# Block forms copied by VectorE, results by tokens, and a check that comes later

## The chip, the cores and the metric

One core of one Trainium2 chip runs the whole program. The metric is device microseconds of one execution, the median of several. TensorE (PE) multiplies into PSUM, VectorE (DVE), ScalarE (ACT) and GpSimd (POOL) do the elementwise work, and SyncE (SP) issues all transfers on one queue.

## The reference

Four batches, 8 heads, 768 tokens, head size 48. A gated linear attention feeds a soft mixture of 8 experts and a dense layer:

```python
f = 1.0 / (1.0 + np.exp(-f_logit))
for t in range(S):
    state = f[:, :, t, :, None] * state + np.einsum('bhd,bhe->bhde', k[:, :, t], v[:, :, t])
    y[:, :, t] = np.einsum('bhd,bhde->bhe', q[:, :, t], state)
...
logits = x @ phi                       # x: y as 3072 tokens x 384
slot_in = softmax(logits, 0).T @ x     # 32 slots, 4 of each expert
slot_out[e] = np.maximum(slot_in[e] @ w1[e], 0.0) @ w2[e]
x = softmax(logits, 1) @ slot_out
...
h = x @ w_in
return (h - np.tanh(h)) @ w_out
```

## The kernel before

**Attention** works in 16 groups g: two pairs of heads, 384 tokens each, cut into three chunks of 128 tokens. A chunk of a group is a step i, 48 in all; g and c are i divided by 3. In q, k and the decays the head size lies on partitions: head 0 of a pair on partitions 0 to 47, head 1 on 64 to 111, and 2 pairs x 3 chunks x 128 tokens in the 768 columns. Six steps share a run of tokens; the first of a run has no old state, the last makes no new one.

`prep` loads f, k, q, makes the running decays (exp, ln on ScalarE, a scan on VectorE, L287, two exps) and multiplies k and q by them, mostly on GpSimd (L260, a helper's line: ks and qs). So that one matmul gives the scores of both heads of a pair, q must also stand in a block form bd: each head's part in columns of its own, zeros in the other's. For groups 0 and 1 VectorE writes it; from group 2 on two transfers within SBUF copy q into it, 48 partitions x 6 pieces of 512 bytes each:

```python
r48 = slice(h * 64, h * 64 + 48)
dma(ring("bd", g)[r48].rearrange("p (x h j) -> p h x j", x=6, h=2)[:, h], Q6[r48])
```

`step` does the rest, by names that the plan uses: P, scores of 128 keys x 128 queries for 2 pairs x 2 heads (L361); ev, their masking out of PSUM by VectorE (L375); K, the transpose of the decayed keys (L370), and kh, ScalarE's copy of it (L379); U, the new state's part, one head at a time in 64 of the 128 stationary columns (L387); sadd and ss, the state's sum and decay on VectorE (L398, L396; L403); Q, the old state times q (L410); Y, values times masked scores, with the values as stationary operand (48 columns, L418), so that results come out with the head size on partitions; yt, ScalarE's copy of them (L423); T, two transposes to tokens on partitions (L428); x, the copy into the activations (L433).

The order of all this is not written by hand: `Plan` takes each operation's engine, cost, dependencies and due time, schedules them in a list, and fixes each engine's order, SyncE's transfers and the prefetches of weights among them. An engine then works strictly in that order. Costs and due times are numbers in the `add` calls.

After attention come token transposes (L1583) and logits, the softmax and slots, the experts (L1866 on) whose weights arrive meanwhile, and the gates. The **dense stage** (`dense`) is a loop of 96 iterations, 6 parts of 512 tokens by 16 blocks: one hidden matmul (L1987), a square on ScalarE (L1993), a product on VectorE (L1994), three output matmuls (L2003). `hook(i, ...)` hangs other work behind iteration i: the conversion of the last weights (va, vb, vc), sums over them (w_mm, w_end), the closing of the first two parts (f_zero), and a check of how large gates and slots are (k_gates to k_ok), which decides whether the fast path's result stands. Of that check `k_gates(0)` is a product on GpSimd, `k_gates(1)` its sum on VectorE, `k_nc` two tiny matmuls with VectorE between them.

Of the kernel before, what the change touches and what calls it, by code (L numbers as in the profile page):

```python
# [173 lines left out]
def arena_map():  # L174
# [8 lines left out]
    for n, w in [("e1_0", 774), ("e1_1", 774), ("rs_0", 774), ("rs_1", 774),  # L183
# [4 lines left out]
                 ("kh_0", 1728), ("kt_0", 256), ("kt_1", 256), ("kt_2", 256), ("yt_0", 256), ("yt_1", 256), ("yt_2", 256),  # L188
# [6 lines left out]
def attention(nc, A, AR, x_all, ident, pcs, BK, plans):  # L195
    amap, _ = arena_map()
    W = {"e1": 774, "rs": 774, "k": 768, "q": 768, "vr": 576, "bd": 1536, "s": 192, "sx": 256, "kt": 256, "yt": 256,
         "pm": 512}
    NB = {"e1": 2, "rs": 2, "k": NKQ, "q": NQ, "vr": 2, "bd": 2, "s": 1, "sx": 3, "kt": 3, "yt": 3, "pm": 3}
# [22 lines left out]
    def vv(i, r, h):  # L222
        gi, c = divmod(i, 3)
        return ring("vr", gi).rearrange("p (c r h e) -> p c r h e", c=3, r=2, h=2)[:, c, r, h]
# [4 lines left out]
    def dma(out, in_):  # L229
        nc.sync.dma_start(out=out, in_=in_)  # L230
# [16 lines left out]
    for i in range(4, 7):  # L247
        add(("zb", i), "dve", 0.36, lambda i=i: memset("dve", BK[i][:, 0:256], 0.0))
# [16 lines left out]
    def prep(g):  # L265
# [63 lines left out]
        for i, x in enumerate(halves):  # L329
            e = EQS.get((g, i), "pool")  # L330
            add(("qs", g, i), e, tt(e, 384), lambda x=x, e=e: mul(e, Q6[:, x], Q6[:, x], X6[:, x]),
                ("q", g), ("e2", g, 0), ("bd", g, 0), ("bd", g, 1))
        if g > 1:
            def bdma():
                for h in range(2):
                    r48 = slice(h * 64, h * 64 + 48)
                    dma(ring("bd", g)[r48].rearrange("p (x h j) -> p h x j", x=6, h=2)[:, h], Q6[r48])

            add(("bd", g), "dma", 0.82, bdma, ("qs", g, 0), ("qs", g, 1), ("P", 3 * g - 4), ("P", 3 * g - 5), ("P", 3 * g - 6))
# [5 lines left out]
    def step(i):  # L345
# [34 lines left out]
        four = lambda a: a.rearrange("p (r h e) -> p r h e", r=2, h=2)[:, :, :, 0:48]  # L380
        ub = BK[4][:, 0:256]
        u = four(ub)
        if not last:
            def mmU():
                for pr in range(2):
                    for h in range(2):
                        nc.tensor.matmul(u[h * 64:h * 64 + 64, pr, h], lhsT=ktk[:, pr, h * 64:h * 64 + 64],  # L387
                                         rhs=vv(i, pr, h), start=pr == 0, stop=pr == 1)

            sn = ring("s", i).rearrange("p (r h e) -> p r h e", r=2, h=2)  # L390
            sp = four(ring("sx", i))
            sp1 = four(ring("sx", i + 1))
            g1, c1 = divmod(i + 1, 3)
            add(("U", i), "pe", 0.4, mmU, ("kh", i), ("v", g), ("sadd", i - 1), ("sadd", i - 2), ("zb", 4))
# [1903 lines left out]
```

## Time and profile before

| | |
|---|---|
| timed runs | 381.83, 384.38, 388.3 us; median 384.38 us |
| the profiled execution's own time | 380.08 us |
| its span, first to last instruction | 378.4 us |
| busy: TensorE, VectorE, ScalarE, GpSimd | 315.3, 240.1, 206.9, 113.3 us |
| mean granted clock of TensorE | 0.951 |
| bytes moved | 67.1 MB, mean 177 GB/s |

All rows are of that one profiled execution, in us from the span's start. Busy shares are means over stages that have different limits, so they are read by stage. A wait is put down to what came last before it ended. In the chain of work that ended last, each piece is what released the next one.

### The profile page before, as it was taken

Reading aid. Unit: us, or ns where it says so; the run is one execution under the profiler, and the core shown is the slowest. Engines: PE = TensorE matmul, PEld = TensorE weight load, DVE = VectorE, ACT = ScalarE, POOL = GpSimd, SP = SyncE. Lnnn points to the kernel's source line nnn. Section 1 sums busy time; section 2 is a strip of 40 time slices with the busy share of each in tenths; the row PEclk is TensorE's granted clock in tenths of the full one; section 3 lists DMA queues with packets and bytes.
Section 4 is the critical chain, followed back from the end, with each engine's and each line's share of the span. In section 5 each row is a group of like instructions: output and inputs, shape, how many; then the busy total and the mean of one; then the engine's idle time right before and its main releaser. Section 6 shows DMA issues by size and latency. Waiting matters only on the chain.

```text
span 378.4 us, 6422 instructions
## 1 busy us (share of the span) xinstructions
PE 315.3 (83%) x2350; PEld 223.6 (59%) x2350; DVE 240.1 (63%) x400; ACT 206.9 (55%) x402; POOL 113.3 (30%) x136
## 2 busy tenths in 40 slices
PE   2988888566469999999989989787957999999991
PEld 1666666455347777777844444654645566778780
DVE  5976676645153744443587993799835469877770
ACT  5655877446351543333477844996541434666651
POOL 7465897342314452000000000345991002000000
PEclk9998999999786999999999999989995999999996
DMA  7978999999999655776418999400000004211202
GB/s 268 323 177 206 270 261 272 272 241 253 260 274 287 172 144 145 224 252 245 193 38 337 425 423 422 193 1 0 0 2 0 0 2 168 83 47 39 83 0 92
DMA packets 26392, 67.10 MB, mean 177 GB/s; under 512 B 3216, under 2 KB 11664, under 8 KB 24688
## 3 DMA queue, kind: packets, MB, share of 16 engines
q1 hardware_dynamic: 26352, 66.61, 57.5%
q8 instruction: 20, 0.33, 0.4%
q14 instruction: 20, 0.16, 0.1%
HBM read 57.75 MB, written 4.72 MB: 165 GB/s over the span
## 4 chain that ended last, share of the span: by engine, by line
PE 40%; DMA 22%; DVE 13%; ACT 8%; POOL 7%; issue 5%; SPq 2%; POOLq 0%; DVEq 0%; ACTq 0%
PE bank L2003 11%; DMA slab_AR<-v 6%; PE bank L361 6%; DMA slab_AR<-wo 5%; DMA slab_AR<-k 4%; DVE r_WA L1994 4%; PE bank L1987 4%; PE bank L418 3%; PE bank L1866 3%; DMA slab_WA<-wi 3%; PE bank L410 3%; POOL slab_AR L1734 3%; POOL slab_AR L260 2%; DMA slab_XA<-f 2%; SPq L230 2%
## 5 line engine op out<-in xcount | busy, mean ns | idle before, releaser
L260 POOL TENSOR_TENSOR slab_AR<-slab_AR 128x384 f32<-128x384 f32 (+1 forms) x65 | 67.1, 1058 | 67.5 <-DMA slab_AR<-k 39.8
L1994 DVE SCALAR_TENSOR_TENSOR r_WA<-bank,slab_AR,slab_WA 128x512 fp32r<-128x512 f32 x96 | 70.4, 749 | 23.8 <-ACT slab_WA L1993 23.3
L1993 ACT ACTIVATE slab_WA<-bank 128x512 f32<-128x512 f32 x96 | 56.9, 598 | 49.2 <-PE bank L1987 49.2
L2003 PE MATMUL bank<-r_WA,r_AR 128*128 128x512 f32 x216 | 66.7, 414 | 12.6 <-DVE r_WA L1994 10.0
L361 PE MATMUL bank<-slab_AR 128*128 128x256 f32 x192 | 54.9, 412 | 3.1 <-DMA slab_AR<-slab_AR 1.6
L2003 PEld LDWEIGHTS bank<-r_WA,r_AR 128*128 128x128 f32 x216 | 40.2, 193 | 28.7 <-DVE r_WA L1994 9.7
L375 DVE TENSOR_TENSOR slab_AR<-bank,slab_AR 128x512 f32<-128x512 f32 x48 | 32.8, 684 | 36.8 <-PE bank L361 36.7
L361 PEld LDWEIGHTS bank<-slab_AR 128*128 128x128 f32 x192 | 34.7, 201 | 10.8 <-issue 3.4
L287 DVE TENSOR_TENSOR_SCAN slab_AR<-slab_XA,slab_AR 128x774 f32<-128x774 f32 (+1 forms) x18 | 31.5, 1750 | 13.0 <-ACT slab_XA L284 10.9
L1987 PE MATMUL bank<-r_AR,r_XA 128*128 128x512 f32 x96 | 38.6, 407 | 0.1
L418 PE MATMUL bank<-slab_AR 128*48 128x128 f32 x384 | 32.1, 290 | 2.5 <-DMA slab_AR<-v 2.5
L428 PE MATMUL bank<-ident,slab_AR 128*128 128x128 f32 x96 | 20.1, 294 | 13.4 <-ACT slab_AR L423 13.1
L433 ACT COPY slab_XA<-bank 128x192 f32<-128x192 f32 x48 | 15.2, 318 | 28.4 <-PE bank L428 28.2
L410 PE MATMUL bank<-slab_AR 128*128 128x128 f32 x160 | 27.1, 294 | 2.1 <-DVE slab_AR L403 2.1
L423 ACT COPY slab_AR<-bank 128x256 f32<-128x256 f32 x48 | 17.9, 372 | 15.2 <-PE bank L418 14.4
L410 PEld LDWEIGHTS bank<-slab_AR 128*128 128x128 f32 x160 | 23.4, 201 | 4.7 <-DVE slab_AR L403 3.0
L418 PEld LDWEIGHTS bank<-slab_AR 128*48 128x48 f32 x384 | 20.0, 128 | 9.9 <-issue 5.2
L387 PE MATMUL bank<-slab_AR 128*64 128x48 f32 x320 | 18.1, 236 | 7.5 <-DMA slab_AR<-v 5.2
L2003 PE MATMUL bank<-r_WA,r_XA 128*128 128x512 f32 x72 | 23.4, 425 | 0.9 <-DVE r_WA L1994 0.9
L290 ACT ACTIVATE slab_AR<-slab_AR 128x774 f32<-128x774 f32 (+1 forms) x18 | 14.0, 778 | 17.8 <-POOL slab_AR L260 10.4
L370 PE MATMUL bank<-ident,slab_AR 128*128 128x128 f32 x80 | 17.9, 308 | 6.7 <-POOL slab_AR L260 6.7
L282 ACT ACTIVATE slab_XA<-slab_XA 128x768 f32<-128x768 f32 (+1 forms) x18 | 14.0, 776 | 17.4 <-DMA slab_XA<-f 7.4
(223 smaller groups left out, 486.1 us busy)
## 6 DMA issues: line engine op xcount, KB each, us to landing
slab_AR<-w SPq DMA_DIRECT2D x5, 1536.0 KB, 7.6
slab_WA<-w SPq DMA_DIRECT2D x12, 512.0 KB, 7.1
slab_AR<-v SPq DMA_DIRECT2D x16, 288.0 KB, 5.7
slab_WA<-wi SPq DMA_DIRECT2D x9, 512.0 KB, 7.7
slab_AR<-wo SPq DMA_DIRECT2D x3, 1536.0 KB, 20.4
out<-slab_WA SPq DMA_DIRECT2D x17, 256.0 KB, 2.1
slab_XA<-f SPq DMA_DIRECT2D x28, 144.0 KB, 6.9
slab_AR<-slab_AR SPq DMA_DIRECT2D x28, 144.0 KB, 5.6
```

The source lines that it names most:

```text
L260: (nc.vector if eng == "dve" else nc.gpsimd).tensor_tensor(out=out, in0=i0, in1=i1, op=ALU.mult)
L287: lambda fs=fs: nc.vector.tensor_tensor_scan(out=ring("rs", g)[:, fs], data0=gt[:, fs], data1=cap[:, fs], initial=0.0, op0=ALU.add, op1=AL ...
L361: nc.tensor.matmul(P.rearrange("p (r h j) -> p r h j", r=2, h=2)[:, pr], lhsT=kv(g)[:, pr, c], rhs=bds[g % 2][R, :, pr, c], start=True, st ...
L375: lambda: nc.vector.tensor_tensor(out=pm, in0=P.rearrange("p (g j) -> p g j", g=4), op=ALU.mult, in1=mask.rearrange("p (g j) -> p g j", g= ...
L387: nc.tensor.matmul(u[h * 64:h * 64 + 64, pr, h], lhsT=ktk[:, pr, h * 64:h * 64 + 64], rhs=vv(i, pr, h), start=pr == 0, stop=pr == 1)
L410: nc.tensor.matmul(y[:, pr], lhsT=ring("sx", i).rearrange("p (r e) -> p r e", r=2)[:, pr], rhs=qv(g)[:, pr, c], start=pr == 0, stop=False)
L418: nc.tensor.matmul(y[h * 64:h * 64 + 48, pr], lhsT=vv(i, pr, h), rhs=pm[:, pr * 2 + h], start=first and pr == 0, stop=pr == 1)
L428: nc.tensor.transpose(out=tb[:, pr * 128:pr * 128 + 128], in_=yt[:, pr * 128:pr * 128 + 128], identity=ident)
L1987: nc.tensor.matmul(h, lhsT=M4[:, fb * 128:fb * 128 + 128], rhs=cT[tg], start=True, stop=True)
L1993: nc.scalar.activation(v, h, AF.Square, scale=THIRD)
L1994: nc.vector.scalar_tensor_tensor(out=r, in0=h, scalar=uu[:, fb:fb + 1], in1=v, op0=ALU.add, op1=ALU.mult)
L2003: nc.tensor.matmul(facc[o], lhsT=w, rhs=r, start=fb == 0, stop=fb == 15 and tg < 2)
```

## The change

1. From group 2 on the block form is written by two copies of 64 partitions x 768 columns on VectorE instead of two transfers; each waits, as the transfers did, for qs and for the score matmuls of the steps that used the buffer before.
2. In Y the masked scores are the stationary operand (128 columns) and the values, 48 columns, the moving one. Results come out with tokens on partitions. Q gets q as the stationary and the state as the moving operand (96 columns). yt and T fall away, with three memsets, the buffer yt and the use of one PSUM bank; x copies straight out of the bank of Y, and Q and Y now wait for x of two steps before.
3. U takes both heads of a pair in one matmul: 128 stationary columns, 96 moving ones. Half of what it makes isn't used. sadd and ss become two operations each, one for each half of the partitions.
4. The check's pieces are hung behind later iterations, k_gates from 18 and 22 to 34 and 39, the others after.
5. The first of the token transposes no longer waits for the last steps, since its bank is free.

```diff
         if g > 1:
-            def bdma():
-                for h in range(2):
-                    r48 = slice(h * 64, h * 64 + 48)
-                    dma(ring("bd", g)[r48].rearrange("p (x h j) -> p h x j", x=6, h=2)[:, h], Q6[r48])
-
-            add(("bd", g), "dma", 0.82, bdma, ("qs", g, 0), ("qs", g, 1), ("P", 3 * g - 4), ("P", 3 * g - 5), ("P", 3 * g - 6))
+            for h in range(2):
+                rr = slice(h * 64, h * 64 + 64)
+                add(("bd", g, h), "dve", 0.5,
+                    lambda h=h, rr=rr: nc.vector.tensor_copy(
+                        ring("bd", g)[rr].rearrange("p (x h j) -> p h x j", x=6, h=2)[:, h], Q6[rr]),
+                    ("qs", g, 0), ("qs", g, 1), ("P", 3 * g - 4), ("P", 3 * g - 5), ("P", 3 * g - 6))
...
                 for pr in range(2):
-                    for h in range(2):
-                        nc.tensor.matmul(u[h * 64:h * 64 + 64, pr, h], lhsT=ktk[:, pr, h * 64:h * 64 + 64],
-                                         rhs=vv(i, pr, h), start=pr == 0, stop=pr == 1)
+                    nc.tensor.matmul(u[:, pr].rearrange("p h e -> p (h e)"), lhsT=ktk[:, pr], rhs=vv(i, pr), start=pr == 0,
+                                     stop=pr == 1)
...
-            add(("U", i), "pe", 0.4, mmU, ("kh", i), ("v", g), ("sadd", i - 1), ("sadd", i - 2), ("zb", 4))
...
+            add(("U", i), "pe", 0.5, mmU, ("kh", i), ("v", g), ("sadd", i - 1, 0), ("sadd", i - 1, 1))
+
+            def add_s(h):
+                rr = slice(h * 64, h * 64 + 64)
+                if first:
+                    nc.vector.tensor_copy(sn[rr], u[rr, :, h])
+                else:
+                    nc.vector.tensor_tensor(out=sn[rr], in0=sp0[rr, :, h], in1=u[rr, :, h], op=ALU.add)
...
+            for h in range(2):
+                add(("sadd", i, h), "dve", 0.2, lambda h=h: add_s(h), ("U", i), ("ss", i - 1, h))
+            for h in range(2):
+                add(("ss", i, h), "dve", 0.25, lambda h=h: scale_s(h), ("sadd", i, h), ("pcs", g1),
+                    ("Q", i - 2), ("zs", (i + 1) % 3))
...
-                    nc.tensor.matmul(y[:, pr], lhsT=ring("sx", i).rearrange("p (r e) -> p r e", r=2)[:, pr],
-                                     rhs=qv(g)[:, pr, c], start=pr == 0, stop=False)
-
-            add(("Q", i), "pe", 0.45, mmQ, ("ss", i - 1), *qsk, ("yt", i - 2))
+                    nc.tensor.matmul(y[:, pr].rearrange("p h e -> p (h e)"), lhsT=qv(g)[:, pr, c],
+                                     rhs=ring("sx", i)[:, 0:192].rearrange("p (r e) -> p r e", r=2)[:, pr], start=pr == 0,
+                                     stop=False)
+
+            add(("Q", i), "pe", 0.5, mmQ, ("ss", i - 1, 0), ("ss", i - 1, 1), *qsk, ("x", i - 2))
...
-                    nc.tensor.matmul(y[h * 64:h * 64 + 48, pr], lhsT=vv(i, pr, h), rhs=pm[:, pr * 2 + h],
-                                     start=first and pr == 0, stop=pr == 1)
-
-        add(("Y", i), "pe", 0.6, mmY, ("ev", i), ("v", g), ("Q", i), ("yt", i - 2), ("Y", i - 1), ("zb", 5), ("zb", 6))
-        yt = ring("yt", i)
-        add(("yt", i), "act", 0.33, lambda: nc.scalar.copy(yt, BK[5 + i % 2][:, 0:256]), ("Y", i), ("T", i - 3))
...
-        add(("T", i), "pe", 0.44, mmT, ("yt", i), ("x", i - 2), "ident")
+                    w = pr * 2 + h
+                    nc.tensor.matmul(y[:, pr, h], lhsT=pm[:, w], rhs=vv(i, pr)[:, h * 48:h * 48 + 48],
+                                     start=first and w == 0, stop=w == 3)
+
+        add(("Y", i), "pe", 0.9, mmY, ("ev", i), ("v", g), ("Q", i), ("x", i - 2), ("Y", i - 1))
...
-        add(("x", i), "act", 0.3, lambda: nc.scalar.copy(dst, four(tb)), ("T", i),
+        add(("x", i), "act", 0.3, lambda: nc.scalar.copy(dst, y.rearrange("p r h e -> p (r h e)")), ("Y", i),
...
-        bank_free = [[("x", 46), ("x", 47)], [("ev", 46)], [("ev", 47)], [("kh", 46)]]
+        bank_free = [[], [("ev", 46)], [("ev", 47)], [("kh", 46)]]
...
-        hook(18, k_gates, 0)
-        hook(22, k_gates, 1)
+        hook(34, k_gates, 0)
+        hook(39, k_gates, 1)
...
-        hook(27, k_nc)
-        hook(34, k_slots, 0)
-        hook(38, k_slots, 1)
-        hook(40, k_bound, 0)
-        hook(45, k_bound, 1)
-        hook(50, k_flags)
-        hook(54, k_ok)
+        hook(44, k_nc)
+        hook(44, k_slots, 0)
+        hook(49, k_slots, 1)
+        hook(51, k_bound, 0)
+        hook(58, k_bound, 1)
+        hook(61, k_flags)
+        hook(64, k_ok)
```

## Rows read from the trace of the kernel before

**Rows 1.** Stretches of the whole run: busy us of each engine, clock, DMA share, GB/s.

```profile
0.00:40.00 40.00, 28.32 (x213) 20.98 (x214) 28.73 (x46) 25.16 (x54) 24.53 (x40) 0.96 0.86 245
40.00:120.00 80.00, 57.65 (x504) 43.88 (x505) 41.01 (x62) 43.47 (x91) 38.96 (x42) 0.91 1.06 263
120.00:178.60 58.60, 57.38 (x526) 44.23 (x525) 29.58 (x56) 23.21 (x64) 14.66 (x16) 1.00 0.65 200
...
202.60:241.50 38.90, 36.35 (x331) 17.58 (x332) 30.27 (x56) 24.22 (x38) 2.59 (x3) 1.00 0.96 392
...
279.60:294.00 14.40, 7.98 (x20) 5.63 (x21) 6.04 (x11) 2.39 (x4) 4.41 (x4) 0.64 0.00 0
```

**Rows 2.** Chain that ended last, 30 to 48 us: start, length, what.

```profile
34.98 4.73 DMA slab_AR<-slab_AR
```

**Rows 3.** DMA issues from 0 to 120 us: count, KB each, median us to landing.

```profile
slab_AR<-slab_AR SPq DMA_DIRECT2D x18, 144.0 KB, 7.5
```

**Rows 4.** Timeline of the dense stage, 276 to 290 us, VectorE and TensorE.

```profile
276.62 0.86 PE L2003 MATMUL bank<-r_WA,r_AR 128*128 128x512 f32 x3
...
277.55 0.86 PE L2003 MATMUL bank<-r_WA,r_AR 128*128 128x512 f32 x3
...
283.00 0.95 DVE L2037 TENSOR_REDUCE slab_AR<-slab_WA 128x24 f32<-128x768 f32 x1 [5.73 <-POOL slab_WA L2035]
...
284.88 1.65 PE L2003 MATMUL bank<-r_WA,r_AR 128*128 128x512 f32 x3 [5.30 <-DVE r_WA L1994]
...
286.88 0.58 PE L2042 MATMUL bank<-ident,chk 128*1 128x128 f32 x2
...
288.61 0.58 PE L2044 MATMUL bank<-chk,slab_AR 1*128 1x1 f32 x2 [1.14 <-DVE chk L2043]
```

**Rows 5.** One stretch of 2 us in which a block form is transferred.

```profile
159.00:161.00 2.00, 2.00 (x20) 1.59 (x20) 0.43 (x2) 1.03 (x4) 0.00 (x0) 1.00 1.08 221
```

**Rows 6.** Waits of the whole run: us in total, times, longest.

```profile
POOL slab_AR L260 <- DMA slab_AR<-k: 39.8, 7, 9.4
...
PE bank L428 <- ACT slab_AR L423: 13.1, 8, 5.5
```

**Rows 7.** Chain that ended last, 135 to 158 us: TensorE's pieces of a step.

```profile
135.66 1.06 PE bank L361 x4
...
140.15 0.22 PE bank L370 x2
...
147.50 0.45 PE bank L410 x4
147.95 0.37 PE bank L387 x8
148.32 0.37 PE bank L428 x2
148.68 0.57 PE bank L418 x8
...
157.01 0.87 PE bank L361 x4
```

**Rows 8.** Timeline of weight loads of the slot sums.

```profile
199.81 1.64 PEld L1702 LDWEIGHTS bank<-slab_AR 128*128 128x128 f32 x14 [0.21 <-DVE slab_AR L1694]
```

**Rows 9.** Three lines: duration in ns, min/median/max, first and last start, shapes.

```profile
L317 DVE COPY slab_AR<-slab_AR x4: 259/289/291, 9.6 to 13.9; 64x256 f32<-64x256 f32 x4
...
L403 DVE TENSOR_TENSOR slab_AR<-slab_AR,pcs x40: 347/358/1082, 14.3 to 171.8; 128x192 f32<-128x192 f32 x40
...
L260 POOL TENSOR_TENSOR slab_AR<-slab_AR x65: 682/952/2462, 6.0 to 147.6; 128x384 f32<-128x384 f32 x60, 128x256 f32<-128x256 f32 x5
```

**Rows 10.** Timeline of VectorE, 202 to 203 us: a 96-wide operation.

```profile
202.26 0.26 DVE L1820 TENSOR_TENSOR slab_AR<-bank,slab_AR 128x96 f32<-128x96 f32 x1
```

**Rows 11.** Costliest groups of the page: ScalarE's copy of values by columns.

```profile
L423 ACT COPY slab_AR<-bank 128x256 f32<-128x256 f32 x48 | 17.9, 372 | 15.2 <-PE bank L418 14.4
```

## What the change was predicted to do

> **What bounds the kernel now.** I read the table of stretches first [rows 1]. Attention runs to about 178.6 us, in two regimes. From 40 to 120 us the DMA engines are full (share 1.06) at only 263 GB/s while TensorE is busy 57.65 of 80 us and its clock falls to 0.91: transfers set the pace. From 120 to 178.6 us TensorE is busy 57.38 of 58.6 us and the DMA share is 0.65: TensorE sets the pace. Between 202.6 and 241.5 us the DMA is full again, at 392 GB/s, with weights that wait for places which earlier stages free; what shortens attention moves this stretch forward and doesn't shorten it. The table's last row is the oddity: from 279.6 to 294.0 us, in the dense stage, TensorE is busy 7.98 of 14.4 us at a granted clock of 0.64.
>
> The chain that ended last agrees for attention. It passes through the block-form transfer itself (4.73 us of waiting for q's second copy) [rows 2]. That transfer is issued 18 times before 120 us, 144 KB each and two for a group: nine groups [rows 3]. The timeline explains the dense stage: VectorE stands 5.73 us at the gates' sum for its product on GpSimd, and TensorE, behind it, 5.30 us [rows 4].
>
> **Transfers.** In 159 to 161 us the transfers of a block form are nearly alone (values follow at the end): share 1.08, 221 GB/s [rows 5]. One group's pair is 2 x 147 KB = 295 KB, so 295/221 = 1.33 us of all sixteen engines, and nine groups 12.0 us before 120 us; the five groups after that cost 6.7 us in a stretch with room and are worth nothing there. In a full queue, work taken out brings all behind it forward, so up to 12 us. I take 11, since the table's row from 0 to 40 us has share 0.86 and two of the nine pairs lie there. Below: nothing, if the order of issue and not the volume sets the pace (rival 1). Above: 20, because two more waits go. P no longer waits for a transfer to land (median 7.5 us [rows 3]), and TensorE no longer stands for ScalarE's copy ahead of the transposes (13.1 us in 8 waits [rows 6]); the new results copy is asked for only two steps later. Both waits lie mostly where transfers rule, so I don't add them. SyncE's queue loses 28 issues and the waits on P and GpSimd before them; loads of keys stand behind those in the queue today, so this too can only help.
>
> The Trainium skill, "DMA: Bandwidth & Descriptors", section "Why small descriptors are slow (HBM only)", says that transfers from SBUF to SBUF don't suffer from small pieces. The 221 GB/s of 512-byte pieces beside 392 GB/s of weights at share 0.96 speaks against it here; by the rule the relief is about half, which is rival 3.
>
> **TensorE per step.** Before, nine score groups start between 135.66 and 157.01 us in the stretch where TensorE is always busy: 21.35/8 = 2.67 us a step [rows 7]. Pieces: scores 0.87 (1.06 where they follow the values), key transpose 0.22, old state 0.45, new state 0.37, two result transposes 0.37, values 0.57. After, everything has 128 stationary columns. Four matmuls of 128 moving columns take 0.45 us today, 0.112 each. That fewer moving columns don't make them shorter is seen in the slot sums, 128x128 weights with 32 moving columns: fourteen loads in 1.64 us, 0.117 each at most [rows 8]; I take 0.112. Values: 8 x 0.112 = 0.90; new state and old state 4 x 0.112 = 0.45 each; the transposes go. Scores are in all six steps of a period, the key transpose and both state terms in five: (6 x 0.87 + 5 x 0.22 + 10 x 0.45 + 6 x 0.90)/6 = 2.70 us. Against 2.67 that is nothing: sum 0. Bounds for 22 steps (58.6/2.67): +7 us if the eight value matmuls take 0.15 each (0.30 a step), -7 if they keep today's 0.07.
>
> **VectorE.** Added: 28 copies of 64x768. Nearest row: 64x256 takes 0.26 to 0.29 us [rows 9]. Three times that is 0.81; with a fixed part of 0.16, as a 192-wide operation has (0.36 less 192 columns at about 1 ns), it is 0.16 + 3 x 0.11 = 0.5. I take 0.5: 14 us in all; upper end 23. Split state operations: four of 64x96 for two of 128x192, 0.26 each [rows 10] against 0.36 [rows 9], so 4 x 0.26 - 2 x 0.36 = +0.3 us in 40 steps, 12 us. VectorE is busy 28.73 + 41.01 + 29.58 = 99 us in attention [rows 1]; 99 + 14 + 12 = 125 us of a new length of about 166 is 75%. I cost it at nothing, covered by TensorE's and the DMA's waits; without that cover it is 26 us (rival 2). What is queued behind a copy that waits for GpSimd's product are the evictions of scores, and TensorE waits for those (rival 4).
>
> **ScalarE** loses 48 copies of 0.37 us [rows 11], off the path until the end: after the last step the chain drops one such copy and one pair of transposes, 0.37 + 0.37 and two hand-overs: 1 us. The freed bank lets two of the 15 token transposes come earlier; 0.
>
> **Gates' check.** In the gap lie four iterations (three matmuls of the output and one of the hidden layer, 0.93 us each at full clock, 276.62 to 277.55 us [rows 4]): 3.7 of 14.4 us. The low clock follows the 5.30 us in which TensorE did nothing, so its cost goes with them. The two small matmuls of the check with their wait, 286.88 to 289.19 us, are moved, not removed: 2.3 us. So 14.4 - 3.7 - 2.3 = 8.4 us; a few tenths come back as VectorE meets the check's reductions while it closes the first parts of the output: 8. The product stays on GpSimd, now at iteration 34, where it has nothing ahead; VectorE wants it five iterations, 4.65 us, later. Bounds: 6 if the moved pieces stretch the crowded iterations 38 to 50, 10 if they hide wholly. If GpSimd were late after all, 5.73 us return at another place.
>
> **Sum.** 11 + 0 + 1 + 8 = 20 us: the profiled execution goes from 380.08 to 360; the timed runs' median is 384.38, so 364.4, and I say 364. A run differs from the next by up to 1.7%, so 2% is what a measurement tells from no change.
>
> **Rivals.**
> 1. Attention doesn't get shorter: the order of issue, fixed by a planner, sets the pace, and loads come no sooner. For it: prefetches of weights keep their places between the loads, and VectorE and GpSimd work to the same order; against it: the share of 1.06 [rows 1]. Then only 1 + 8: 375; with the upper cost of TensorE's values, 382, so that half of it lies within 2%.
> 2. VectorE becomes the bound. The state product of 128x192 takes 0.36 at the median and 1.08 at the most, GpSimd's product 0.95 and 2.46 [rows 9]: they hold each other up. If each of 28 copies waits for one product, 28 x 0.95 = 27 us more, VectorE's 125 becomes 152 and fills 92% of 166; a gain of 3 is left of 11: 372. The Trainium skill, "SBUF — State Buffer", section "Who interferes with whom", has this as an exclusive lock: an fp32 copy within SBUF takes the pair of ports that GpSimd needs, and the later of the two blocks fully. By that rule the copies are worse neighbours than the transfers, which touch no engine's port; the maxima above agree with it.
> 3. Block-form transfers cost no more per byte than weights: 295/392 = 0.75 us a group, 6.8 in all, relief 6: 369.
> 4. Slower: VectorE's queue stands at the copies. GpSimd waits 39.8 us in 7 waits for keys [rows 6]; today SyncE and P bear that, with the copies VectorE does, and evictions of earlier steps stand behind. If 27 us of it stop TensorE, attention grows by 27 - 11 = 16: 384.4 + 16 - 9 = 391.4, with a little more than that slower by 2%. It decides from 1.4 us of standing for each of 14 groups, 20 us, on. Against it: VectorE is idle nearly half of 40 to 120 us, and P would have waited for the same product.
> 5. More than the sum: the removed waits count as well, attention 20 shorter: 355.
>
> **How the numbers follow.** Forecast, 358 to 369 with a likeliest 364: 0.48. Rival 5, down to 350: 0.15, a little of it below. Rival 3: 0.05. Rival 2: 0.14. Rival 1: 0.12, half of it within 2%. Rival 4: 0.06. The range 350 to 376 leaves out about 0.04 below, and 0.06 + 0.06 and some of rival 2 above. Faster by over 2% means under 376.7: 0.48 + 0.15 + 0.05 + 0.11 + 0.06 = 0.85; within 2%: 0.09; slower: 0.06.
>
> **What would show it.** Right: the transfers from slab_AR to slab_AR are gone; the full stretch ends about 11 us sooner; the first token transposes start near 167 instead of 178.6 us; the step spacing in the busy stretch stays near 2.7; VectorE's 5.73 us wait and the low clock after 279.6 us are gone, with the rest of the dense stage as long as before. Wrong: a spacing of 3 us or more (value matmuls dearer), VectorE busy over 85% of attention, copies of block forms far over 0.5 us, or VectorE's longest waits naming GpSimd.

## The result, and the profile after

The changed kernel took 367.2 us (median of four runs, 362.8 to 372.0) beside 384.9 us for the kernel before on the same chip. The ratio is 0.949 with a 95% interval of 0.935 to 0.962: faster. (This ratio and those below leave disturbed runs out; the medians don't, so the two differ by up to 1.3%.) The forecast was 364.0 with a range of 350 to 376. Its profiled execution took 365.4 us, a span of 363.7; the one before took 380.1, a span of 378.4.

The sum of the forecast was 20 us of profiled time; 14.7 came. Where they came is read from the timelines. The table gives start times in us, and the last column the length of a stretch; "H1" and so on are the dense stage's 96 hidden-layer matmuls, counted from one.

| | end of attention | H1 | H31 | H37 | H50 | H96 | end | H37 to H50 |
|---|---|---|---|---|---|---|---|---|
| before | 176.9 | 241.3 | 279.2 | 296.8 | 318.8 | 366.2 | 378.4 | 22.0 |
| changed | 173.4 | 236.4 | 274.2 | 280.9 | 306.1 | 353.2 | 363.7 | 25.2 |
| gained so far | 3.5 | 4.9 | 5.0 | 15.9 | 12.7 | 13.0 | 14.7 | |

So attention gave 3.5 us instead of 11 (5.9 in a second profile of the changed kernel, below); from its end to the first dense matmul 1.4; the gap before H37 10.9, of which 3.2 were given back by H50; the end 1.7. That last part isn't the change's: its code is the same, and from H96 to the end the profile of before took 12.2 us, all the others 9.7 to 11.8. The first token transposes do start at 168.5 us instead of 177.4, as forecast, but that is a trap: in the new order three of the 15 units come before the last values' products, and the first logits are only 7.3 us earlier.

The stretches of the changed kernel that answer to [rows 1], with the same columns:

```profile
core 0: us, PE busy (x) PEld busy (x) DVE busy (x) ACT busy (x) POOL busy (x), PEclk, DMA share, GB/s
0.00:40.00 40.00, 29.07 (x158) 24.77 (x159) 30.95 (x55) 22.73 (x45) 23.08 (x39) 0.96 0.76 233
40.00:120.00 80.00, 66.67 (x463) 60.26 (x462) 66.63 (x128) 37.37 (x75) 39.02 (x44) 0.95 0.90 253
120.00:173.40 53.40, 51.23 (x373) 47.65 (x373) 40.45 (x87) 18.99 (x43) 11.71 (x17) 0.97 0.51 162
```

The DMA share from 40 to 120 us is 0.90 where it was 1.06: the transfers have left the bound. VectorE has come in their place: 66.6 of 80 us there, where [rows 1] has 41.0, and 138.0 of 173.4 over attention. From 20 to 60 us, seen finer, it is busy 36.9 of 40 us, where it was 28.5 before. First the changed kernel, then the one before:

```profile
20.00:40.00 20.00, 16.47 (x106) 14.00 (x106) 17.59 (x29) 10.98 (x21) 9.40 (x13) 0.91 0.62 176
40.00:60.00 20.00, 16.25 (x115) 14.18 (x114) 19.31 (x33) 9.43 (x18) 13.17 (x14) 1.00 0.83 247
...
20.00:40.00 20.00, 16.59 (x138) 12.51 (x138) 13.77 (x18) 12.96 (x27) 12.02 (x15) 0.91 0.80 198
40.00:60.00 20.00, 18.39 (x176) 14.13 (x177) 14.72 (x20) 14.56 (x30) 18.05 (x17) 1.00 1.06 267
```

What VectorE and TensorE do in attention (groups by line and shape from 0 to 180 us; busy us, then mean ns of one, then idle time before it and what ended it):

```profile
L401 DVE TENSOR_TENSOR slab_AR<-slab_AR,pcs 64x96 f32<-64x96 f32 x80 | 33.6, 420 | 2.3
...
L382 PE MATMUL bank<-slab_AR 128*128 128x96 f32 x160 | 26.1, 289 | 4.7 <-DMA slab_AR<-v 2.0 <-ACT slab_AR L288 1.4 <-issue 1.1
...
L335 DVE COPY slab_AR<-slab_AR 64x768 f32<-64x768 f32 x28 | 19.4, 693 | 1.5 <-POOL slab_AR L258 1.1
...
L396 DVE TENSOR_TENSOR slab_AR<-slab_AR,bank 64x96 f32<-64x96 f32 x64 | 16.0, 250 | 7.4 <-PE bank L382 5.9
...
L394 DVE COPY slab_AR<-bank 64x96 f32<-64x96 f32 x16 | 4.0, 252 | 3.1 <-PE bank L382 2.7
```

The state's scaling by halves (L401) takes 0.42 us each where the forecast had 0.26, and the copies (L335) 0.69 where it had 0.5. The state alone is 33.6 + 16.0 + 4.0 = 53.6 us of VectorE; the same groups before were 18.1 + 11.1 + 2.8 = 32.0 us:

```profile
L403 DVE TENSOR_TENSOR slab_AR<-slab_AR,pcs 128x192 f32<-128x192 f32 x40 | 18.1, 453 | 1.7
...
L398 DVE TENSOR_TENSOR slab_AR<-slab_AR,bank 128x192 f32<-128x192 f32 x32 | 11.1, 347 | 14.2 <-PE bank L387 13.5
...
L396 DVE COPY slab_AR<-bank 128x192 f32<-128x192 f32 x8 | 2.8, 356 | 9.6 <-PE bank L387 9.4
```

The forecast had +12 for this, the trace has +21.6.

Waits of the whole run that answer to [rows 6] (us in total, times, longest):

```profile
POOL pcs L293 <- ACT slab_AR L288: 38.8, 8, 7.3
...
ACT slab_AR L288 <- DVE slab_AR L285: 19.0, 9, 3.1
...
POOL slab_AR L258 <- DMA slab_AR<-k: 5.1, 4, 2.7
```

GpSimd's wait for keys has fallen from 39.8 to 5.1 us. It now waits for ScalarE's exponentials, these for VectorE's scan (L285), and the scan stands in VectorE's queue behind masks, state operations and copies. Each of the three hands its wait to the next, and VectorE is the one of them that is full.

In the dense stage, the timeline that answers to [rows 4]:

```profile
276.44 1.48 POOL L2030 TENSOR_TENSOR slab_WA<-slab_AR 128x768 f32<-128x768 f32 x1
...
280.33 0.73 PE L1998 MATMUL bank<-r_WA,r_AR 128*128 128x512 f32 x2 [0.41 <-DVE slab_WA L2007]
...
296.35 0.94 DVE L2032 TENSOR_REDUCE slab_AR<-slab_WA 128x24 f32<-128x768 f32 x1
...
302.47 0.38 PE L2037 MATMUL bank<-ident,chk 128*1 128x128 f32 x2
302.68 0.74 DVE L2020 SCALAR_TENSOR_TENSOR slab_XA<-bank,slab_AR,slab_XA 128x512 f32<-128x512 f32 x1
303.34 1.40 DVE L1989 SCALAR_TENSOR_TENSOR r_WA<-bank,slab_AR,slab_WA 128x512 fp32r<-128x512 f32 x2
304.66 0.27 DVE L2038 TENSOR_REDUCE chk<-bank 1x1 f32<-1x128 f32 x1
304.98 0.38 PE L2039 MATMUL bank<-chk,slab_AR 1*128 1x1 f32 x2 [2.13 <-DVE chk L2038]
```

VectorE's sum (L2032) no longer waits: its product was ready 18 us before, and TensorE has no wait over 0.41 us between H31 and H37. But the row of maxima (L2037 to L2039) now comes right behind the two closing sums of `f_zero`. The last of their six VectorE operations of 0.7 us (L2020), and two of the loop's products that stand behind it (L1989), are still to run. TensorE issues its second matmul only when VectorE has reduced the first: 2.13 us of standing, and that is most of the 3.2 us given back.

### The profile page after: what moved, and what is told of

The parts are those of the page before. It is cut to its first block, busy times and chain, and to the rows that moved or that the text cites. A ratio compares the mean times of both kernels' runs of the same rounds, so it can differ in the third digit from the quotient of the medians.

```text
span 363.7 us, 5953 instructions
## 1 busy us (share of the span) xinstructions
PE 314.9 (87%) x2094; PEld 243.7 (67%) x2094; DVE 279.0 (77%) x505; ACT 193.8 (53%) x354; POOL 108.8 (30%) x136
## 4 chain that ended last, share of the span: by engine, by line
PE 49%; DVE 25%; DMA 11%; ACT 8%; issue 4%; SPq 1%; POOL 1%; POOLq 0%; DVEq 0%; ACTq 0%
PE bank L1998 14%; PE bank L359 6%; PE bank L422 6%; DVE slab_AR L285 4%; PE bank L1982 4%; DMA slab_AR<-w 4%; DVE r_WA L1989 4%; PE bank L412 3%; DVE slab_AR L401 3%; DVE slab_AR L335 3%; PE bank L382 3%; DVE slab_AR L373 2%; PE bank L1861 2%; PE bank L1578 2%; DMA slab_AR<-k 2%
## 5 line engine op out<-in xcount | busy, mean ns | idle before, releaser
L1989 DVE SCALAR_TENSOR_TENSOR r_WA<-bank,slab_AR,slab_WA 128x512 fp32r<-128x512 f32 x96 | 70.7, 749 | 21.7 <-ACT slab_WA L1988 20.9
L258 POOL TENSOR_TENSOR slab_AR<-slab_AR 128x384 f32<-128x384 f32 (+1 forms) x65 | 63.1, 997 | 33.6 <-ACT slab_AR L288 13.0
L1998 PE MATMUL bank<-r_WA,r_AR 128*128 128x512 f32 x216 | 64.8, 404 | 8.4 <-DVE r_WA L1989 6.1
L359 PE MATMUL bank<-slab_AR 128*128 128x256 f32 x192 | 57.3, 425 | 2.2 <-POOL slab_AR L258 1.0
L422 PE MATMUL bank<-slab_AR 128*128 128x48 f32 x384 | 50.4, 276 | 1.9 <-DVE slab_AR L373 1.9
L422 PEld LDWEIGHTS bank<-slab_AR 128*128 128x128 f32 x384 | 49.5, 198 | 3.7 <-DVE slab_AR L373 2.8
L373 DVE TENSOR_TENSOR slab_AR<-bank,slab_AR 128x512 f32<-128x512 f32 x48 | 33.1, 691 | 12.5 <-PE bank L359 11.4
L359 PEld LDWEIGHTS bank<-slab_AR 128*128 128x128 f32 x192 | 36.3, 210 | 6.4 <-POOL slab_AR L258 1.2
L412 PE MATMUL bank<-slab_AR 128*128 128x96 f32 x160 | 26.4, 290 | 10.8 <-DVE slab_AR L401 4.4
L401 DVE TENSOR_TENSOR slab_AR<-slab_AR,pcs 64x96 f32<-64x96 f32 x80 | 33.6, 420 | 2.3
L412 PEld LDWEIGHTS bank<-slab_AR 128*128 128x128 f32 x160 | 23.2, 201 | 15.9 <-DVE slab_AR L401 4.5
L285 DVE TENSOR_TENSOR_SCAN slab_AR<-slab_XA,slab_AR 128x774 f32<-128x774 f32 (+1 forms) x18 | 29.8, 1656 | 4.4 <-ACT slab_XA L282 4.1
L382 PE MATMUL bank<-slab_AR 128*128 128x96 f32 x160 | 26.1, 289 | 4.7 <-DMA slab_AR<-v 2.0
L382 PEld LDWEIGHTS bank<-slab_AR 128*128 128x128 f32 x160 | 22.9, 204 | 6.1 <-issue 4.3
L377 ACT COPY slab_AR<-bank 128x256 f32<-128x256 f32 x40 | 14.7, 371 | 19.4 <-PE bank L368 19.4
L368 PE MATMUL bank<-ident,slab_AR 128*128 128x128 f32 x80 | 16.6, 294 | 6.8 <-POOL slab_AR L258 6.8
```

Source lines behind the costliest of these rows:

```text
L258: (nc.vector if eng == "dve" else nc.gpsimd).tensor_tensor(out=out, in0=i0, in1=i1, op=ALU.mult)
L285: lambda fs=fs: nc.vector.tensor_tensor_scan(out=ring("rs", g)[:, fs], data0=gt[:, fs], data1=cap[:, fs], initial=0.0, op0=ALU.add, op1=AL ...
L359: nc.tensor.matmul(P.rearrange("p (r h j) -> p r h j", r=2, h=2)[:, pr], lhsT=kv(g)[:, pr, c], rhs=bds[g % 2][R, :, pr, c], start=True, st ...
L373: lambda: nc.vector.tensor_tensor(out=pm, in0=P.rearrange("p (g j) -> p g j", g=4), op=ALU.mult, in1=mask.rearrange("p (g j) -> p g j", g= ...
L382: nc.tensor.matmul(u[:, pr].rearrange("p h e -> p (h e)"), lhsT=ktk[:, pr], rhs=vv(i, pr), start=pr == 0, stop=pr == 1)
L401: nc.vector.tensor_tensor(out=sp1[rr, :, h], in0=sn[rr], in1=dc, op=ALU.mult)
```

## Experiments

Each group of runs was taken on one chip with the kernel before beside it; medians and ranges are of one group. The first group's chip is another than that of the second and third, so differences across groups are rougher than those within one. The theory: the transfers' relief was real, and VectorE, which the forecast costed at nothing, took a part of it back. The rivals: the transfers were worth little, and TensorE's new work or the order of issue decides.

### First group of runs (kernel before: 382.1 us)

**The check alone moved.** Kernel before, with the new places for the check only:

```
-        hook(18, k_gates, 0)
-        hook(22, k_gates, 1)
...
+        hook(34, k_gates, 0)
+        hook(39, k_gates, 1)
...
```

> The kernel before with the gates' check alone moved to its later places; the attention is that of before. The forecast's own term for this is 8 us (376.4, ratio 0.979; bounds 6 to 10). What the profile of the changed kernel showed is the same size: between the 30th and 36th dense iteration 10.9 us went, and about 3 us were given back between the 46th and 52nd, where the moved row of maxima now waits. Theory: 7 to 9 us faster, the dense part's loss of 5.73 us and the low clock gone, everything ahead of the dense part as before. Rival: the gap in before had a part that only the old attention's timing made; then under 5 us.

375.8 us (366.6 to 377.4), 6.3 less by medians. The stretches H31 to H37 and H37 to H50:

```profile
283.37:290.08 6.71, 6.05 (x25) 4.43 (x24) 5.59 (x8) 4.56 (x9) 3.75 (x3) 1.00 0.00 0
290.08:315.40 25.32, 22.71 (x135) 13.95 (x134) 16.16 (x27) 8.74 (x15) 1.04 (x1) 0.99 0.17 63
```

6.71 and 25.32 us where before had 17.6 and 22.0: 10.9 gone, 3.3 given back, the clock 1.00 and 0.99. These are the changed kernel's lengths to 0.2 us, behind an attention of before. So this part is worth 7.6 us wherever attention ends, and the rival falls. The same attention ended at 181.3 us here and at 176.9 in the profile of before; that scatter, some 4 us here and 6 in a pair further below, bounds what one profile can say of attention.

**The copies alone.** Kernel before with VectorE's copies in the places of the transfers:

```
-                    r48 = slice(h * 64, h * 64 + 48)
-                    dma(ring("bd", g)[r48].rearrange("p (x h j) -> p h x j", x=6, h=2)[:, h], Q6[r48])
+                    rr = slice(h * 64, h * 64 + 64)
+                    nc.vector.tensor_copy(ring("bd", g)[rr].rearrange("p (x h j) -> p h x j", x=6, h=2)[:, h], Q6[rr])
```

> The kernel before with one part of the change alone: the block form copied by VectorE (28 copies) in place of the transfers, everything else, the orders of the other engines too, as before. Theory A (the relief of the transfers is real, and VectorE's added time takes part of it back): VectorE goes from 99 to about 117 us in the attention, which here has whole state operations instead of halves; the attention ends 5 to 8 us sooner, ratio 0.98 to 0.987. Theory B (the block-form transfers cost next to nothing, what the changed kernel won in the attention is TensorE's work): within 2 us of before. Theory C (the copies hold up the queue): slower by 2 us or more.

369.6 us (366.7 to 371.6), 12.5 less by medians; the ratio is 0.980 (0.958 to 1.003), 7.5 us less, and wide because runs of before scatter from 374.3 to 390.6 here. Its four executions all lie below the 19 of before. Attention ends at 167.2 us, 9.7 sooner than in the profile of before, and nearer the forecast's 167 than the whole change's 173.4. Theory A holds, at its own size by the ratio and larger by medians; B and C fall. In the profiles one part of the change does more for attention than all of it.

**The transfers again.** Changed kernel, block form by transfers, all else kept:

```
-                    lambda h=h, rr=rr: nc.vector.tensor_copy(
+                    lambda h=h, rr=slice(h * 64, h * 64 + 48): dma(
```

> The changed kernel with the block form written by transfers again, in the places of the copies; all other engines keep their order. Its ratio to before is to be set beside the changed kernel's, 0.949 (the interval 0.935 to 0.962). Theory A (relief real, VectorE takes part back): the attention ends 4 to 6 us later than the changed kernel's, ratio 0.960 to 0.965. Theory B (block-form transfers cost next to nothing, VectorE's copies cost something): ratio 0.945 or less, faster than the changed kernel. Theory D (the split state operations on VectorE are what ate the gain, not the copies): ratio near 0.975, since the transfers cost their full 11 us again and the halves stay.

379.8 us (377.4 to 385.6), ratio 1.005 (0.998 to 1.012): later than every theory's number, nearest to D. With the check worth 7.6 us, the new arrangement of the matmuls and the state must cost some 5 us by medians, 9 by the ratio, when the transfers are there. Its attention ended at 188.7 us, 7 to 12 later than the old arrangement's with the same transfers. Its stretch from 40 to 120 us:

```profile
40.00:120.00 80.00, 69.31 (x417) 62.94 (x417) 53.02 (x98) 38.32 (x75) 35.08 (x41) 0.82 1.03 250
```

DMA full again (1.03), VectorE at 53.0 us, and TensorE's clock down to 0.82 in the mean though it is busy 69.3 of 80 us.

**No block form written** in the changed kernel:

> The changed kernel without the block-form copies of the groups from 2 on (left out: the key-query products of these groups use an old block form, so the output is not the reference's); all orders are kept. This is the price of the copies themselves. In the changed kernel they are 28 of 0.69 us, 19.4 us of VectorE's time, in an attention where VectorE is busy 95% of 20 to 60 us. Theory A (VectorE sets the pace in the middle of the attention): 4 to 7 us faster than the changed kernel, ratio 0.930 to 0.938, and VectorE's share in 20 to 60 us falls to 80%. Theory B (the attention is now bound by TensorE and the scan's chain, the copies lie beside it): within 2 us of the changed kernel.

8090 us: with such numbers the kernel's own check turned to its general path, and the run says nothing of the copies. The last kernel below leaves the transfers out instead, with the check's answer written in.

### Second group of runs (kernel before: 383.4 us)

**Whole state operations.** Changed kernel; only the new keys' products and the state's operations are those of before (with the bank of zeros that they need), and all engines' orders are planned anew:

```
-                    nc.tensor.matmul(u[:, pr].rearrange("p h e -> p (h e)"), lhsT=ktk[:, pr], rhs=vv(i, pr), start=pr == 0,
-                                     stop=pr == 1)
+                    for h in range(2):
+                        nc.tensor.matmul(u[h * 64:h * 64 + 64, pr, h], lhsT=ktk[:, pr, h * 64:h * 64 + 64],
+                                         rhs=vv(i, pr)[:, h * 48:h * 48 + 48], start=pr == 0, stop=pr == 1)
...
-            for h in range(2):
-                add(("ss", i, h), "dve", 0.25, lambda h=h: scale_s(h), ("sadd", i, h), ("pcs", g1),
-                    ("Q", i - 2), ("zs", (i + 1) % 3))
+            add(("ss", i), "dve", 0.4, scale_s, ("sadd", i), ("pcs", g1), ("Q", i - 2), ("zs", (i + 1) % 3))
```

> The changed kernel with the new keys' products and the state's operations as they were before (four 64-row products, one whole addition and one whole scaling per step, one more bank of zeros); the copies, the results by tokens and the check's places stay as changed; the orders are planned anew. In the changed kernel's attention the halves took VectorE 53.6 us (80 scalings of 0.420, 64 additions of 0.250, 16 copies of 0.252), the whole operations before took 32.0; and the pairs' products took TensorE 26.1 us against 18.1. Theory E (the halves are what took the copies' gain back: the run with the copies alone ended its attention at 166.8 us, the changed kernel at 173.2): 4 to 7 us faster than the changed kernel run beside it. Rival F (the results by tokens, 384 products of 48 columns with 128-column weights, took it back through TensorE and its clock): within 2 us of the changed kernel, attention's end at 172 to 175. Rival G (nothing of these, the scatter of runs): attention's end between.

**Copies and check, old arrangement:** kernel before with the two edits of the first group.

> The kernel before with two parts of the change: the block form copied by VectorE, and the gates' check later; the new TensorE arrangement (results by tokens, keys by pairs, halves) is left as before. The copies alone gave 369.6 us, the check alone 375.8, against 382.1 on that chip: if they add, 382.1 - 12.5 - 6.3 = 363 us. Theory E or F (the new arrangement costs 4 to 7 us in the attention beside the copies): 2 to 6 us faster than the changed kernel. Rival G (the arrangement is worth nothing either way): the same time as the changed kernel within 2 us.

**Copies on ScalarE** in the changed kernel:

```
-                    lambda h=h, rr=rr: nc.vector.tensor_copy(
+                    lambda h=h, rr=rr: nc.scalar.copy(
```

> The changed kernel with the 28 block-form copies issued on ScalarE instead of VectorE, all orders kept. In the changed kernel VectorE was busy 154.9 of the first 200 us and ScalarE 94.4; the copies took VectorE 19.4 us (0.69 each, longest 1.33 where GpSimd worked beside). A copy of 768 columns on ScalarE should take about 0.85 us, the time of its 768-column exponentials (0.846), so 24 us and no slow ones. Theory A (VectorE sets the pace in 20 to 60 us): 3 to 6 us faster than the changed kernel. Rival B (scan, exponentials and GpSimd's products form one chain, in which ScalarE's added time stands as well): within 2 us, or slower by up to 4 where copies stand ahead of exponentials in ScalarE's queue.

**The changed kernel again:**

> The changed kernel unaltered, so that the other three are compared with it on one chip. Its first runs had a median of 367.2 us (362.8 to 372.0); the kernel before had 384.9 there and 382.1 (374.3 to 390.6) on the other chip. Expected 363 to 368.

| | us | attention ends | ratio to before (95%) |
|---|---|---|---|
| changed again | 362.5, 367.7, 370.0 | 171.0 | 0.962 (0.952 to 0.972) |
| copies and check alone | 362.9 (361.6 to 366.7) | 167.1 | 0.950 (0.940 to 0.960) |
| ScalarE's copies | 359.6 (358.4 to 361.9) | 168.2 | 0.940 (0.932 to 0.948) |
| whole state operations | 358.5 (353.8 to 362.0) | 166.2 | 0.935, of medians |

A fourth execution of the changed kernel took 1038 us, for which nothing here gives a cause; it is left out, and 367.7 is the median of the other three.

Theory E holds: with whole state operations the kernel is 9 us faster than the changed one, and the ranges don't overlap. The clock isn't all of it: at a mean granted clock of 0.981 the changed kernel took 362.5 us, the one with whole state operations 357.7 at 0.985 and 353.8 at 0.980. So the pairs with their halves, and the order planned for them, are a loss. The third group has a smaller number for it, 6 us, and there the same attention ended at 172.2 us, so attention's end in one profile wouldn't have shown it.

The kernel with copies and check alone can't be told from the changed one: 4.8 us less by medians, but the ranges overlap, and its ratio, 0.950, is that of the changed kernel's first runs, 0.949. Here rival G stands. The kernel with whole state operations, which has the results by tokens as well, is 4.4 us under it, with ranges that just touch, and a kernel of the third group makes that 1.6. So the results by tokens, and the order planned for them, show no cost, and rival F falls; that they are a gain is likely but not shown. The state groups with whole operations:

```profile
L402 DVE TENSOR_TENSOR slab_AR<-slab_AR,pcs 128x192 f32<-128x192 f32 x40 | 22.7, 566 | 0.8
L386 PE MATMUL bank<-slab_AR 128*64 128x48 f32 x320 | 18.3, 237 | 2.6 <-issue 1.6 <-DMA slab_AR<-v 0.9
...
L397 DVE TENSOR_TENSOR slab_AR<-slab_AR,bank 128x192 f32<-128x192 f32 x32 | 11.0, 345 | 7.3 <-PE bank L386 6.7
L395 DVE COPY slab_AR<-bank 128x192 f32<-128x192 f32 x8 | 2.8, 352 | 2.4 <-PE bank L386 2.3
```

36.5 us of VectorE instead of 53.6, and TensorE's new-state products 18.3 us instead of 26.1 (twice as many, each with 64 columns of weights). The experiment undoes both, so how the 9 us divide between VectorE and TensorE isn't shown by it. ScalarE's copies relieve VectorE alone, with every order kept, and give 8 us by medians, again with ranges that don't overlap, at clocks of 0.963 to 0.974 (8 and 3 by the ratios, beside 0.962 and 0.949). Their line in that kernel (duration of one in ns, minimum/median/maximum, then first and last start):

```profile
L335 ACT COPY slab_AR<-slab_AR x28: 816/829/833, 27.7 to 151.2; 64x768 f32<-64x768 f32 x28
```

0.83 us each, 23.2 us in all, on an engine with room; on VectorE they were 525/556/1334 in the changed kernel. VectorE is then busy 31.0 us from 20 to 60 us instead of 36.9:

```profile
20.00:40.00 20.00, 16.23 (x107) 14.18 (x105) 15.07 (x29) 12.45 (x23) 8.74 (x12) 0.91 0.61 174
40.00:60.00 20.00, 16.66 (x116) 15.21 (x116) 15.89 (x28) 15.63 (x26) 14.99 (x14) 0.96 0.96 258
```

Theory A holds, with its own size or more; rival B falls. This is the experiment that shows VectorE as a bound.

### Third group of runs (kernel before: 382.8 us)

**Whole state and ScalarE's copies together:**

> The changed kernel with the whole state operations and four 64-row key products of the kernel before, and the block-form copies on ScalarE. Alone, the whole state operations gave 358.5 us and ScalarE's copies 359.6, beside 367.7 for the changed kernel (383.4 before). VectorE is then down to about 100 of the first 160 us. If VectorE was what both relieved, they don't add in full: 354 to 357 us. If each relieved a chain of its own (the state's chain from step to step; the queue ahead of the masks), they add: 350 us.

**Whole state, row of maxima in two pieces:**

```
-    def k_nc():
-        b, c = nxt(), nxt()
+    def k_nc(x):
+        b = nxt()
+        if x == 0:
...
+            return
+        c = b
...
-        hook(44, k_nc)
+        hook(44, k_nc, 0)
+        hook(47, k_nc, 1)
```

> The kernel with whole state operations (358.5 us) with the check's row of maxima in two calls: its first product stays at iteration 44, the second, which waits for VectorE's reduction of the first, goes to iteration 47. In the dense part of every kernel with the check moved, 25.2 us pass from the 36th to the 49th first product, 22.0 before the move; TensorE stands 2.13 us at this second product, behind VectorE's queue. Theory: the 22 come back, 2 to 3 us faster, 355.5 to 356.5. Rival: the 3 us are the cost of the check's other instructions on VectorE (0.94 for the sums of squares and what follows) and of the backlog that the six zero-order sums leave; then within 1 us of 358.5.

**All three:**

> All three together: whole state operations, block-form copies on ScalarE, the row of maxima in two calls. Expected 351 to 354 us, the two attention edits not adding in full and the split row giving 2 to 3; if none of these adds to the whole state operations, 358.

**Before without the block-form transfers,** nothing in their place:

```
-            add(("bd", g), "dma", 0.82, bdma, ("qs", g, 0), ("qs", g, 1), ("P", 3 * g - 4), ("P", 3 * g - 5), ("P", 3 * g - 6))
+            add(("bd", g), "dma", 0.82, lambda: None, ("qs", g, 0), ("qs", g, 1), ("P", 3 * g - 4), ("P", 3 * g - 5), ("P", 3 * g - 6))
...
+        nc.vector.memset(one(7), 1.0)
         nc.vector.tensor_copy(K["ok"], one(7))
```

> The kernel before without the block-form transfers, and with nothing in their place: the key-query products of the groups from 2 on use an old block form, and the check's answer is written as good in any case (one more small write), since these numbers would fail it. All orders are kept. This is the relief of the transfers by itself, the forecast's first term: 11 us with bounds of 0 and 20. Theory A: the copies alone on VectorE gave 12.5 us, and 20 us of VectorE's time in that arrangement cost little, so the relief by itself is 12 to 16 us: 367 to 371. Rival B (the copies cost about 5 us there too): 17 to 19 us, 364 to 366. Rival H (transfers were never in the way, and the copies' gain was one of earlier block forms): under 6 us, 377 or more.

| | us | attention ends | H37 to H50 | ratio to before (95%) |
|---|---|---|---|---|
| whole, ScalarE | 362.6 (355.4 to 366.6) | 175.8 | 25.2 | 0.935 (0.921 to 0.950) |
| whole, two pieces | 358.8 (356.8 to 361.2) | 172.2 | 22.7 | 0.937 (0.928 to 0.947) |
| all three | 354.3 (352.6 to 357.2) | 166.2 | 22.7 | 0.928 (0.916 to 0.939) |
| before, no transfers | 365.1 (363.8 to 366.6) | 166.2 | 22.0 | 0.955 (0.945 to 0.964) |

The two pieces do what they should: the stretch is 22.7 us in both kernels that have them, 25.2 to 25.8 in all others with the check moved, and in the last kernel's timeline neither matmul has a wait:

```profile
295.14 0.38 PE L2034 MATMUL bank<-ident,chk 128*1 128x128 f32 x2
...
297.32 0.27 DVE L2035 TENSOR_REDUCE chk<-bank 1x1 f32<-1x128 f32 x1
...
299.10 0.38 PE L2038 MATMUL bank<-chk,slab_AR 1*128 1x1 f32 x2
```

The time of the second kernel doesn't show it, and by its total alone the rival would hold: its attention ended 6 us later than the same attention did in the group before (172.2 against 166.2). The first kernel is inconclusive: its executions lie 11 us apart, and in the profiled one TensorE's granted clock was 0.70 from 20 to 60 us, where the second and third had 0.96 and 0.92. All three together are the fastest kernel of the study, 28.5 us under before and, by their ratios, 0.928 against the changed kernel's 0.949 and 0.962. The third differs from the second by the engine of the copies alone and is 4.4 us faster, with ranges that just touch. Without the 2.5 us of the row in two pieces it would be 356.8, inside the 354 to 357 expected if VectorE is what both attention edits relieve: they don't add in full.

The last one is the forecast's first term by itself: 17.8 us less than before by medians, 14 to 21 by the interval of the ratio. Between the two profiled executions (366.6 and 380.1) it is 13.5, of which 10.8 at attention's end and 2.5 behind H96, where the code is the same. By medians that is rival B's number, but theory A's 12 to 16 isn't excluded. The copies on VectorE gave 12.5 of the 17.8, so by medians they cost 5.3 even in the old arrangement; as the two come from two chips, and attention ended at 167.2 and 166.2, this is not shown.

## Why the prediction came out

That the total was right is partly luck: one step was taken too small, another at nothing, and the two errors cancel. By differences of medians, in us:

| step of the sum | forecast | measured | from |
|---|---|---|---|
| transfers' relief | 11 (0 to 20) | 17.8 (14 to 21) | before without transfers |
| VectorE: copies | 0 | -5.3; -4.4 to -8.1 | copies alone, less that; copies on ScalarE |
| VectorE: halves, with the pairs' products | 0 | -6 to -9 | whole state operations |
| TensorE's step and results by tokens, with the tail | 0 + 1 | +1.6 to +4.4 | whole state against copies and check |
| gates' check | 8 | 6.3 (7.6 by stretches) | check alone |

17.8 - 5.3 - 9.2 + 4.4 + 6.3 is 14.0; the changed kernel gained 17.7 and 15.7 in its two groups. So the table is good to a few us in each row, and the signs are firmer than the sizes. (The second kernel of the third group, corrected by the 2.5 us of its row in two pieces, would be 361.3: the halves' loss is then 6, and the results by tokens give 1.6.)

**Transfers.** The mechanism was right: the share fell from 1.06 to 0.90, the transfers from slab_AR to slab_AR are gone, the chain's DMA part went from 22% to 11%. The size was taken too small, by medians and by the transfers' own time. The price came from a quiet stretch: counted packet by packet in the trace of before, the 512-byte pieces took 35 ns each from 159 to 161 us (where a third of the bytes behind the 221 GB/s, 147 of 442 KB, weren't theirs), but 46 ns from 40 to 120 us. So the nine pairs took 14.6 us of all sixteen engines, not 12.0. Whether the pieces' low rate comes from their size or from the 48 partitions that a transfer reaches, no run here tells apart. Rival 5's reason, that the waits removed count as well, fits the rest; the profiled pair alone, 11 us up to H96, would have left the term as it stood. Rival 3 (6 us) and rival 1 (nothing) fall.

**VectorE** is the step that failed: "I cost it at nothing, covered by TensorE's and the DMA's waits". It was priced at undisturbed times and weighed as a mean over attention, 75%. The undisturbed times were right (0.25 us for a half's scaling, 0.55 for a copy, with GpSimd idle); beside GpSimd's products they were 0.72 in the mean and up to 1.33. The mean came out at 80%, below the 85% that was to show the forecast wrong; the stretch that counts, 20 to 60 us, at 92%. Rival 2 named the mechanism and the lock with GpSimd, and in part it happened: with copies and halves undone together the kernel is 10.9 us faster than the changed one (356.8 as above against 367.7), which is not the whole gain. Rival 2 named the copies only; the halves of the state, on the path from each step to the next, cost about as much. Rival 4 didn't come: VectorE waited for GpSimd 1.1 us in all at the copies, as L335 above shows.

**TensorE per step** was right. TensorE's pieces in the changed kernel's chain, from a first score group to the tenth:

```profile
146.17 0.89 PE bank L359 x4
147.06 0.42 PE bank L412 x4
...
147.70 0.42 PE bank L382 x4
...
151.87 0.82 PE bank L422 x8
...
169.13 0.86 PE bank L359 x4
```

Nine steps take 2.55 us each, against 2.70 forecast. Only eight of the values' products lie among them, and one unit of token transposes (0.46 us); with nine products and without the transposes it would be 2.59. Values for one step are mostly 0.82 to 0.85 us in the chain, not 0.90; each state product 0.42 to 0.49 beside 0.45. By busy time the pairs' products take 26.1 us of TensorE instead of 18.1; in the chain it is 0.42 to 0.45 for 0.37, which was in the sum and was balanced there by the transposes that go.

**Gates' check.** The 10.9 us of the gap are more than the 8.4 reckoned, as the two small matmuls left it too; the forecast had "a few tenths" coming back where they land, and it was 3.2 us. Its reason was VectorE closing the first parts; the wait is TensorE's, for that VectorE. 7.6 net beside 8.

## What to carry to other kernels

When transfers stop being the bound, look for the next engine in the very stretch that they ruled, slice by slice, not in its share of the whole stage: 80% of a stage was 92% of the 40 us that mattered. Price an operation beside the neighbours that it will have: both prices taken from quiet rows, the transfers' and VectorE's, were too low. An operation halved in size isn't half as long (0.25 us against 0.36 here), so splitting one is an added cost on a busy engine, to be tried apart from the edits that it comes with: here it lost 6 to 9 us, half or more of the 12.5 that the copies had gained. A matmul that needs another engine's answer to the one just before it wants other work between the two, and the answering engine's backlog is the place to look before choosing where.

## What the runs showed of the hardware

VectorE's operations beside GpSimd's products lengthen or don't, by where their inputs are. In the changed kernel's timeline:

```profile
84.33 0.54 DVE L401 TENSOR_TENSOR slab_AR<-slab_AR,pcs 64x96 f32<-64x96 f32 x2
...
124.43 1.84 POOL L258 TENSOR_TENSOR slab_AR<-slab_AR 128x384 f32<-128x384 f32 x2
124.57 1.82 DVE L401 TENSOR_TENSOR slab_AR<-slab_AR,pcs 64x96 f32<-64x96 f32 x2
```

The same pair of scalings takes 0.54 us alone and 1.82 beside GpSimd. Of the 80, taken one by one from the trace, the 45 with GpSimd idle take 0.253 us in the mean, and the 23 wholly beside it 0.716. The additions of the same shape with one input in PSUM (L396) take 0.249 and 0.252, the masks from PSUM 0.691 in both cases. The Trainium skill, "SBUF — State Buffer", section "Who interferes with whom", says just this: a VectorE instruction with two SBUF inputs contends with a GpSimd instruction that reads SBUF, one with at most one such input and outside the two-port modes doesn't. The trace agrees. ScalarE's copies had no slow ones beside the same products (0.816 to 0.833 us).

TensorE's clock fell most in one kernel without TensorE being idle for long: with the transfers back in the new arrangement it was 0.82 in the mean from 40 to 120 us, at 69.3 of 80 us busy, where the changed kernel had 0.95 at 66.7. It did fewer matmuls in that time, 417 instead of 463. It stood at the lower of its two levels, 1.2 GHz, from 40 to 45 and from 90 to 95 us (granted clock 0.50), and most of 65 to 70 us (0.53). Before the falls at 65 and 86 us TensorE had stood 1.0 and 1.4 us; in the changed kernel it stood 1.5 and 1.4 us, at 98 and 108 us, and the clock stayed at 2.4 GHz. What lowers it there stays open.
